# Lending query slots, input tiles and accumulators to a heap of exponential blocks

## The chip, the core and the metric

The kernel runs on one core of one Trainium2 chip. A core has five engines that run side by side and wait for each other by semaphores: TensorE (PE, matrix products, with its weight loads shown as PEld), ScalarE (ACT, functions of single elements), VectorE (DVE), GpSimd (POOL) and SyncE (SP, which here issues DMAs). Compute engines work on SBUF, 128 partitions; matmuls write PSUM, eight banks of 128x512 fp32. The metric is the time of one execution on the device, in microseconds.

## What is computed

Four layers with a residual each: `x = x + A(LN(x)); x = x + B(LN(x)); x = x + A(LN(x)); x = x + B(LN(x))`, for 2048 rows of 512 elements, with the same weights in both A layers and in both B layers.

```python
def A(x, wq, wk, wv, wo):          # 32 query heads of 16, ONE key and value head
    q = heads(x @ wq); k = x @ wk; v = x @ wv
    p = softmax(q @ k.T * 16 ** -0.5)          # 32 x 2048 x 2048
    return merge(p @ v) @ wo
def B(x, wqkv, wo):                # linear attention, 32 heads of 16
    q, k, v = split(x @ wqkv)
    phi = lambda t: where(t > 0, t + 1, exp(t)) + 1e-6
    kv = phi(k).T @ v; z = phi(k).sum(rows)
    return merge(phi(q) @ kv / (phi(q) @ z + 1e-6)) @ wo
```

Layers 0 and 2 are of kind A, layers 1 and 3 of kind B. Nearly all of the work is the softmax of the A layers.

## The kernel before

**A planner writes the order.** The program isn't a loop over tiles but a small event simulation (`Planner`) that runs while the program is built. Every piece of a layer is a Python generator that waits for flags, takes a PSUM bank or a buffer from a pool, and then calls `op` with an engine, an assumed duration, a priority and the keys it reads and writes. The planner gives each engine the ready operation of least priority number and so fixes each engine's order; at the end it emits these orders with semaphore waits that follow from the keys. The assumed durations only shape the order. On the chip each engine works through its list in that order.

**Layers of kind A.** The 2048 rows are 16 tiles of 128. `ln_tile` normalizes a tile and transposes it into `xnT` (features on partitions), by DMA for tiles 4 to 15 and by TensorE for the first. `a_k`, `a_v` and `a_q` project keys, values and queries (`mm4` at line 966 issues 16 matmuls for a tile's queries, `copy_flex` at line 780 copies the bank to `QT`, one slot of 128x512 for each tile). The keys lie in `KM` twice, each copy masked to half of the rows, so that a matmul over 32 rows gives the scores of one head: "par" is the half, j the group of 32 rows.

A segment (`Seg`) is a query tile and a half: 16 key tiles times four groups j, 64 blocks of 128 keys by 512 columns (four heads' worth of 128 queries). A layer has 32 segments' worth of blocks, 2048; the first tiles of a layer are cut into shorter pieces (`E0`, `E2`), so that work can begin before all keys are there, and their sums are kept in `sacc`, one fp32 accumulator for each tile and half. `act_stream` walks the segments in rounds. A round takes a set of three PSUM banks; up to three score matmuls (line 1051) fill them, and ScalarE makes one exponential of two or three banks (line 1240). Where two are enough for ScalarE, the third bank goes to VectorE (`dve_split`), and where a bank is spare VectorE gets one more (`dve_open`). VectorE does the exponential as integer arithmetic on the bits of a bf16 (line 1344). Four such blocks are a chunk; GpSimd adds a constant to a chunk three times (`int64_add`, line 1386), which shifts the approximation's phase, and the four versions are weighted and summed by four value matmuls (`VW`) in place of one (`V`, both line 1105). VectorE blocks are allowed from the eighth key tile on (`KGATE`), are picked from the back of a segment, and only if enough blocks lie ahead.

**The heap.** All exponentials, VectorE blocks and shifted copies live in `W`, a tile of 72 blocks of 128x512 bf16 handed out by `Heap_`, lowest number first. A block is held until its value matmul. Four rules look at how many are free: ScalarE's `take` needs its blocks and four more (`RES`), a new VectorE chunk more than 8 (`FBO`), a shift that isn't urgent more than 16 (`FBS`), and a value matmul with fewer than four column groups is held back while 14 or more are free (`LOW`).

**Value matmuls and the end of a segment.** Value matmuls go segment by segment into bank 6, four column groups at a time. Then VectorE copies the bank to `sacc` (lines 1407 and 1409), TensorE transposes it (1429), VectorE divides (1436, 1440), and `epilogue` transposes, multiplies by `wo` and adds to `x_sb`. Fillers (line 1150) are matmuls with zeros that TensorE runs when it has nothing else to do.

**Layers of kind B** run tile by tile under the attention of their neighbours: `tile_` normalizes into `xnT` and projects keys and values, `q_` projects queries into `QT` and applies phi (line 1516 on ScalarE, 1517 and 1519 on VectorE), `kv_`/`kvt` build the products, `main`/`main3` finish a tile. phi(k) lies in `pk`, which is a view of `sacc` 2 to 5.

**When queries are projected.** In layer 0 all tiles are projected as soon as their input is there. In layer 2 tiles 5 to 15 wait for a segment's end (`QHOLD`, `QHC`). In layer 1 tiles 4 to 13 wait until layer 0's exponentials are all planned (`QLATE`, flag `exps`).

## Time and profile before

| what | value |
|---|---|
| time, median of 3 runs | 1393.46 us (1390.98 to 1452.55) |
| the profiled execution | 1391.23 us, of which the span is 1389.3 us |
| busy: TensorE / ScalarE / VectorE / GpSimd | 1344.2 / 1347.3 / 1216.5 / 1033.0 us |
| granted TensorE clock, mean | 0.999 |
| DMA | 20.58 MB, mean 15 GB/s |

The span runs from the first to the last instruction of the profiled execution. A row of a group gives the line, the engine and operation, the tile written and read, the number of instructions, then their busy time together, the mean time of one in ns, and the idle time of the engine just before them with what ended most of it. Instructions overlap in their engine's pipeline, so the busy time of a group is less than the count times the mean. A row of waits gives the total in us, the number of waits and the longest. A row of windows gives the stretch, its length and the busy time with the number of instructions for each engine, then the granted clock, the DMA share and GB/s.

### The profile page before, as it was taken

The page shows a single profiled execution, that of the slowest core. Times are in us where ns is not written, and L with a number is a line of the kernel's source. Part 1 is how long each engine was busy: PE and PEld are TensorE (multiplying, and loading weights), DVE is VectorE, ACT ScalarE, POOL GpSimd, SP SyncE. Part 2 cuts the span into 40 slices and gives each one's busy share as a digit, 9 for nine tenths or more (in the row PEclk, how much of TensorE's full clock was granted, in tenths as well). Part 3 has the DMA queues.
Part 4 walks back from the last instruction along what each step waited for, and adds up shares of the span by engine and source line. Part 5 has one row for each costly group of instructions (what it writes and reads, how often), then busy time and mean ns, then how long its engine had stood idle before and what let it go on. Part 6 is the DMA issues. An engine that isn't in the chain of part 4 may idle for free.

```text
span 1389.3 us, 38426 instructions
## 1 busy us (share of the span) xinstructions
PE 1344.2 (97%) x15092; PEld 465.4 (33%) x15092; DVE 1216.5 (88%) x2184; ACT 1347.3 (97%) x1543; POOL 1033.0 (74%) x1031
## 2 busy tenths in 40 slices
PE   8999999999999999999999999999999999999998
PEld 5422222232222222233632333333333322223335
DVE  8889888898889988897889988988898899888977
ACT  8999999999999999999799999999999999999996
POOL 1489998778979998776005878867888799977770
PEclk9999999999999999999999999999999999999999
DMA  4300000000000000000021000000000000000001
GB/s 108 93 6 5 6 6 20 6 13 2 10 9 6 5 6 13 2 1 3 5 51 36 5 5 9 21 6 6 13 6 9 5 6 5 6 13 2 2 2 62
DMA packets 52465, 20.58 MB, mean 15 GB/s; under 512 B 46144, under 2 KB 51776, under 8 KB 52288
## 3 DMA queue, kind: packets, MB, share of 16 engines
q1 hardware_dynamic: 51232, 18.10, 5.7%
q8 instruction: 122, 2.00, 0.6%
q14 instruction: 55, 0.45, 0.1%
q10 hardware_dynamic: 1056, 0.03, 0.0%
HBM read 5.28 MB, written 2.10 MB: 5 GB/s over the span
## 4 chain that ended last, share of the span: by engine, by line
PE 52%; ACT 29%; DVE 9%; issue 7%; POOL 1%; DMA 1%; SPq 0%; ACTq 0%; DVEq 0%; POOLq 0%
ACT W L1240 28%; PE ps L1105 20%; PE ps L1051 17%; PE ps L786 6%; DVE W L1344 5%; PE ps L966 3%; PE ps L1429 2%; PE ps L1150 2%; POOL W L1386 1%; ACT phE L1516 1%; DVE phE L1517 1%; DVE sacc L1407 1%; DVE xn L884 1%; DMA x_sb<-in_A_x_dram 1%; DVE st L871 0%
## 5 line engine op out<-in xcount | busy, mean ns | idle before, releaser
L1240 ACT ACTIVATE W<-ps 128x1024 bf16<-128x1024 f32 (+1 forms) x1332 | 1287.5, 1157 | 11.5 <-PE ps L1051 8.4
L1386 POOL INT64_ADD W<-W x999 | 1027.4, 1041 | 314.7 <-DVE W L1344 156.8
L1344 DVE TENSOR_SCALAR W<-ps 128x512 int16<-128x512 f32 x1332 | 868.8, 683 | 121.8 <-PE ps L1051 106.5
L1105 PE MATMUL ps<-W,VW 128*32 128x512 bf16 x5328 | 562.4, 384 | 7.5 <-DVE sacc L1407 7.1
L1051 PE MATMUL ps<-QT,KM 32*128 32x512 bf16 x4096 | 520.7, 385 | 23.9 <-ACT W L1240 12.9
L1105 PE MATMUL ps<-W,V 128*32 128x512 bf16 x2764 | 447.7, 384 | 0.0
L1051 PEld LDWEIGHTS ps<-QT,KM 32*128 32x128 bf16 x4096 | 130.5, 91 | 508.0 <-ACT W L1240 444.6
L1105 PEld LDWEIGHTS ps<-W,VW 128*32 128x32 bf16 x5328 | 133.7, 94 | 177.6 <-issue 115.8
L1105 PEld LDWEIGHTS ps<-W,V 128*32 128x32 bf16 x2764 | 108.0, 94 | 71.2 <-issue 46.7
L786 PE MATMUL ps<-wqkv,xnT 128*128 128x512 bf16 (+1 forms) x272 | 76.1, 371 | 1.7 <-DVE sacc L1519 1.5
L1150 PE MATMUL ps<-QT,V 128*32 128x512 bf16 (+4 forms) x278 | 74.1, 333 | 0.9 <-DVE QT L780 0.8
L1516 ACT ACTIVATE phE<-ps 128x512 bf16<-128x512 f32 (+1 forms) x66 | 43.5, 663 | 6.8 <-PE ps L966 6.7
L1407 DVE COPY sacc<-ps 128x512 f32<-128x512 f32 x64 | 43.6, 681 | 6.0 <-PE ps L1105 5.9
L1429 PE MATMUL ps<-identF,sacc 128*128 128x128 f32 x256 | 46.0, 292 | 1.6 <-DVE sacc L1519 0.8
L871 DVE BATCH_NORM_STATS2 st<-x_sb 128x6 f32<-128x512 bf16 x60 | 40.5, 680 | 0.6 <-DMA x_sb<-in_A_x_dram 0.3
L884 DVE TENSOR_SCALAR xn<-x_sb,mv,rs 128x512 bf16<-128x512 bf16 x64 | 35.6, 571 | 2.2 <-ACT rs L862 2.0
L966 PE MATMUL ps<-xnT,wqkv 128*128 128x128 bf16 x512 | 37.4, 220 | 0.0
L1517 DVE TENSOR_SCALAR phE<-phE 128x512 bf16<-128x512 bf16 (+1 forms) x66 | 33.2, 506 | 4.5 <-ACT phE L1516 4.1
L786 PE MATMUL ps<-wo,OT 128*128 128x512 bf16 x120 | 36.0, 384 | 0.9 <-DVE QT L1519 0.5
L966 PE MATMUL ps<-xnT,wq 128*128 128x128 bf16 x464 | 35.2, 220 | 0.0
L1429 PEld LDWEIGHTS ps<-identF,sacc 128*128 128x128 f32 x256 | 27.6, 142 | 19.9 <-issue 14.3
L1150 PEld LDWEIGHTS ps<-QT,V 128*32 128x32 bf16 x278 | 22.7, 95 | 29.7 <-issue 15.6
(140 smaller groups left out, 599.0 us busy)
## 6 DMA issues: line engine op xcount, KB each, us to landing
out_dram<-x_sb SPq DMA_DIRECT2D x16, 128.0 KB, 1.7
x_sb<-in_A_x_dram SPq DMA_DIRECT2D x6, 256.0 KB, 5.4
wqkv<-in_B_wqkv_dram SPq DMA_DIRECT2D x1, 1536.0 KB, 7.9
xnT<-xn SPq DMA_TRANSPOSE x46, 2.5
x_sb<-in_A_x_dram SPq DMA_DIRECT2D x4, 128.0 KB, 2.2
wq<-in_A_wq_dram SPq DMA_DIRECT2D x1, 512.0 KB, 4.2
wo<-in_A_wo_dram SPq DMA_DIRECT2D x1, 512.0 KB, 4.1
wo<-in_B_wo_dram SPq DMA_DIRECT2D x1, 512.0 KB, 8.8
```

Source lines behind the costliest of these rows:

```text
L786: return e.matmul(dst, lhsT=l, rhs=r, start=(k == 0), stop=(k == len(pairs) - 1))
L884: op({DV: (0.325, lambda e: e.tensor_scalar(out=xn[:, i, :], in0=x_sb[:, t, :], scalar1=mv[:, t, 0:1], scalar2=rs[:, t:t + 1], op0=ALU.sub ...
L966: ins = e.matmul(dst[:, g * P:(g + 1) * P], lhsT=lhs(g, k), rhs=rhs(k), start=(k == 0), stop=(k == FT - 1))
L1051: return e.matmul(bank(b), lhsT=KM[r, sg.par, kt * P:(kt + 1) * P], rhs=QT[r, sg.t, :], start=True, stop=True)
L1105: ins = e.matmul(ps[32 * j:32 * j + 32, ACC * 512:(ACC + 1) * 512], lhsT=V[:, kt, :] if w is None else VW[:, kt, w, :], rhs=ap, start=(k = ...
L1150: o = op({PE: (n / 2400.0, lambda e: e.matmul(ps[32 * j:32 * j + 32, b * 512:b * 512 + n], lhsT=V0[:], rhs=QT[:, sg.t, 0:n], start=st, sto ...
L1240: ex = op({AC: (EXO + 0.4267 * n, lambda e, n=n, s_=s_, p_=p_: e.activation(ws_(p_), ps[:, s_ * 512:(s_ + n) * 512], ACTF.Exp, scale=EXPSC ...
L1344: o = op({DV: (0.602, lambda e: e.tensor_scalar(out=dst.bitcast(I16), in0=bank(b), scalar1=VB, scalar2=VLO, op0=ALU.add, op1=ALU.max))}, w ...
L1386: o = op({PO: (512 * m * PSR + PSO, lambda e, g_=g_, f_=f_: e.int64_add(ws_(g_).bitcast(I64), ws_(f_).bitcast(I64), step))}, reads=wk_(f_) ...
L1407: o = op({DV: (0.6, lambda e, src=src: e.tensor_copy(src, bank(ACC)))}, writes=[B_(ACC), key], prio=0.0, lat=0.15)
L1429: o = op({PE: (0.12, lambda e, c=c: e.transpose(ps[:, b * 512 + c * P:b * 512 + (c + 1) * P], src[:, c * P:(c + 1) * P], identF[:]))}, rea ...
L1516: op({AC: (0.07 + n / 1200.0, lambda e: e.activation(phE[:, i, 0:n], bank(b, n), ACTF.Exp))}, reads=[B_(b)], writes=[("phE", i)], prio=pr ...
```

## The change

All of the lendable memory is put into one tile with the heap. `W` grows from 72 blocks to 108: 16 are the query slots (`QT` becomes a view of them), 16 the normalized inputs (`XT`, which replaces `xnT` and has one block of four 128x128 pieces for each tile, so that a tile's inputs lie together), and four are two of the eight fp32 accumulators (units 6 and 7; `sacc` shrinks to six). The memory in total is the same.

A lendable block is at home, in use by its owner, or lent. `lend` hands it to the heap, `lend_after` does so when a flag is there and its last readers are done, and `recall` takes it back: if it is free at once, else when the heap releases it, asked every 0.2 us of the planner's time.

- Layer 0: query slots 4 to 15 and the four accumulator blocks are lent from the start. A tile's queries are now projected only when the value matmuls of segment 2t+2 are all issued, six segments ahead of its first own segment. Slots 4 to 13 are lent again after the tile's last segment. The accumulator blocks are recalled when the layer's exponentials are planned.
- Layer 1's queries recall their slots. When a tile of layer 1 is finished, slots 5 to 15 are lent until layer 2's queries.
- Layer 2: the accumulators 6 and 7 are lent once they are transposed for the last time. Inputs of layer 3's tiles 0 to 13 are lent after their last projection.

The constants of the heap's rules stay as they are.

```diff
     def free(self, heap, blocks):
-        heap.free.update(blocks)
+        heap.home.update(heap.back.intersection(blocks))
+        heap.free.update(set(blocks) - heap.back)
...
 class Heap_:
     def __init__(self, n):
-        self.n = n
+        self.n = n + 2 * T + 4
         self.free = set(range(n))
+        self.home = set(range(n, self.n))
+        self.back = set(self.home)
...
+LEND0 = range(4, 16)
+QLEAD = 6
+XLEND = 14
...
-    xnT = sb("xnT", [P, FT, S], BF16)
-    QT = sb("QT", [P, T, D], BF16)
...
-    W = sb("W", [P, NW, 512], BF16)
+    W = sb("W", [P, NW + 2 * T + 4, 512], BF16)
+    QT = W[:, NW:NW + T, :]
+
+    XT = W[:, NW + T:NW + 2 * T, :].rearrange("p t (f s) -> p t f s", f=FT)
+    SB0 = NW + 2 * T
...
-    sacc = sb("sacc", [P, 8, 512], FP32)
+    sacc = sb("sacc", [P, 6, 512], FP32)
+
+    def acc_(u):
+        if u < 6:
+            return sacc[:, u, :], [("sacc", u)]
+        b = SB0 + 2 * (u - 6)
+        return W[:, b:b + 2, :].rearrange("p a b -> p (a b)").bitcast(FP32), [("W", b), ("W", b + 1)]
...
             yield ("flag", ("K", L, T - 1))
             if QHC is not None:
                 yield ("flag", ("pv", L, QHC + 2 * (t - QHOLD[L][0])))
-        yield from until(("xnT", t))
+        if L == 0 and t in LEND0:
+            i = 2 * len(E0) + 2 * (t - 2) - QLEAD
+            if i >= 0:
+                yield ("flag", ("pv", L, i))
+        yield from recall(NW + t)
+        yield from until(XK_(t))
...
+    def lend(b):
+        heap.back.discard(b)
+        heap.home.discard(b)
+        pl.free(heap, [b])
+
+    def lend_after(key, b):
+        def g():
+            yield ("flag", key)
+            yield ("ops", list(pl.readers.get(("W", b), ())) + pl.ws(("W", b)))
+            lend(b)
+        pl.process(g())
+
+    def recall(b):
+        heap.back.add(b)
+        if b in heap.free:
+            heap.free.discard(b)
+            heap.home.add(b)
+        while b not in heap.home:
+            yield ("sleep", 0.2)
+
+    def shares():
+        for t in LEND0:
+            lend(NW + t)
+        for i in range(4):
+            lend(SB0 + i)
+        yield ("flag", ("exps", 0))
+        for i in range(4):
+            yield from recall(SB0 + i)
...
             if sg.submitted == sg.total:
                 pl.flag(("pv", L, sg.i))
+                if sg.last and sg.par and L == 0 and sg.t in QLATE[1]:
+                    lend_after(("pv", L, sg.i), NW + sg.t)
...
             if a_ is not None:
                 pl.give_after(as_pool, a_, [o])
+            elif L == 2 and sg.unit >= 6:
+                for i in range(2):
+                    lend_after(("pv", L, sg.i), SB0 + 2 * (sg.unit - 6) + i)
...
             if t in QLATE[L]:
                 yield ("flag", ("exps", L - 1))
-            yield from until(("xnT", t))
+            yield from recall(NW + t)
+            yield from until(XK_(t))
...
             pl.give_after(bq_pool, s_, [o])
+            if L == 3 and t < XLEND:
+                yield ("flag", ("kvin", L, t))
+                lend_after(("pkin", L, t), NW + T + t)
             pl.flag(("bq", L, t))
...
             pl.flag(("x", L, t))
+            if t in QHOLD[2]:
+                lend_after(("x", L, t), NW + t)
```

Everywhere else, `xnT[:, k, t * P:(t + 1) * P]` becomes `XT[:, t, k, :]` and the keys `("xnT", t)` and `("QT", t)` become the heap's `("W", b)`. A key matmul over several tiles reads `XT[:, t0:t0+n, ft, :]`, n pieces of 128 columns.

More of the change, by code (lines that the diff above doesn't have):

```diff
@@ L752, in setup @@
         yield ("flag", ("Q", 0, 1))
-        yield from until(("QT", 0))
+        yield from until(QK_(0))
         pool_op(lambda e: e.memset(identF[:], 0.0), ["identF"], prio=1.0)
@@ L926, in a_v @@
             yield ("flag", ("xnT", L, t))
-        yield from until(*[("xnT", t) for t in ts])
+        yield from until(*[XK_(t) for t in ts])
         b = yield ("acq", banks, prio)
@@ L945, in a_k @@
             yield ("flag", ("xnT", L, t))
-        yield from until(*[("xnT", t) for t in ts])
+        yield from until(*[XK_(t) for t in ts])
         n = P * len(ts)
@@ L949, in a_k @@
         b = yield ("acq", banks, prio)
-        mm(bank(b, n), [(wkr[:, ft, :], xnT[:, ft, cs]) for ft in range(FT)], [("xnT", t) for t in ts] + ["wkr"], b, prio, 4 * (0.02 + n / 2500.0))
+        mm(bank(b, n), [(wkr[:, ft, :], XT[:, ts[0]:ts[0] + len(ts), ft, :]) for ft in range(FT)], [XK_(t) for t in ts] + ["wkr"], b, prio, 4 * (0.02 + n / 2500.0))
         last = None
@@ L1424, in norm @@
             yield ("flag", ("oslot", L, sg.t))
-            yield from until(key)
+            yield from until(*key)
             b = yield ("acq", banks, pr)
@@ L1561, in tile_ @@
                 yield ("flag", ("kv", L, t // 4 - 2))
-            yield from until((EB if t in ECRIT else "xnT", t))
+            yield from until((EB, t) if t in ECRIT else XK_(t))
             if t in ECRIT:
@@ L1570, in tile_ @@
             b = yield ("acq", banks, pr)
-            mm(bank(b), [(xnT[:, ft, t * P:(t + 1) * P], wqkv[:, ft, D:2 * D]) for ft in range(FT)], [("xnT", t), "wqkv"], b, pr, 0.9)
+            mm(bank(b), [(XT[:, t, ft, :], wqkv[:, ft, D:2 * D]) for ft in range(FT)], [XK_(t), "wqkv"], b, pr, 0.9)
             pl.process(phi_k(t, b, sl, pr))
@@ L1574, in tile_ @@
             b = yield ("acq", banks, pr)
-            mm(bank(b), [(xnT[:, ft, t * P:(t + 1) * P], wqkv[:, ft, 2 * D:3 * D]) for ft in range(FT)], [("xnT", t), "wqkv"], b, pr, 0.9)
+            mm(bank(b), [(XT[:, t, ft, :], wqkv[:, ft, 2 * D:3 * D]) for ft in range(FT)], [XK_(t), "wqkv"], b, pr, 0.9)
             src, dst = bank(b).rearrange("p (h d) -> p h d", d=DH), va_v[:, sl, :, 0:DH]
@@ L1693, in den3 @@
                 yield ("flag", ("bq", L, t))
-            yield from until(*[("QT", t) for t in ts], *ZK)
+            yield from until(*[QK_(t) for t in ts], *ZK)
             i = yield ("acq", rd_pool, pr)
@@ L1837, in main @@
                 yield ("flag", ("xnT", 2, MW[t]))
-                yield from until(("xnT", MW[t]))
+                yield from until(XK_(MW[t]))
             i = yield ("acq", ob_pool, pr)
```

64 lines of the change are left out of this document (35 added, 29 removed).

## The prediction

> **What bounds the kernel now.** I first read the page's busy times, its chain and its costliest groups, to see which engine paces the attention layers.
>
> ```profile
> PE 1344.2 (97%) x15092; PEld 465.4 (33%) x15092; DVE 1216.5 (88%) x2184; ACT 1347.3 (97%) x1543; POOL 1033.0 (74%) x1031
> ...
> PE 52%; ACT 29%; DVE 9%; issue 7%; POOL 1%; DMA 1%; SPq 0%; ACTq 0%; DVEq 0%; POOLq 0%
> ACT W L1240 28%; PE ps L1105 20%; PE ps L1051 17%; PE ps L786 6%; DVE W L1344 5%; PE ps L966 3%; PE ps L1429 2%; PE ps L1150 2%; POOL W L1386 1%; ACT phE L1516 1%; DVE phE L1517 1%; DVE sacc L1407 1%; DVE xn L884 1%; DMA x_sb<-in_A_x_dram 1%; DVE st L871 0%
> ...
> L1240 ACT ACTIVATE W<-ps 128x1024 bf16<-128x1024 f32 (+1 forms) x1332 | 1287.5, 1157 | 11.5 <-PE ps L1051 8.4
> L1386 POOL INT64_ADD W<-W x999 | 1027.4, 1041 | 314.7 <-DVE W L1344 156.8
> L1344 DVE TENSOR_SCALAR W<-ps 128x512 int16<-128x512 f32 x1332 | 868.8, 683 | 121.8 <-PE ps L1051 106.5
> L1105 PE MATMUL ps<-W,VW 128*32 128x512 bf16 x5328 | 562.4, 384 | 7.5 <-DVE sacc L1407 7.1
> ```
>
> The softmax exponentials are shared out in blocks of 128x512, 4096 in all. ScalarE (L1240) takes two or three blocks in one instruction. VectorE (L1344) takes single blocks, 1332 of them, and GpSimd (L1386) makes three shifted copies of every four. A VectorE block therefore needs 5328/1332 = 4 value matmuls where a ScalarE block needs one. TensorE and ScalarE are both 97% busy, so the share must be read by stage. The next answer gives the busy time of every engine over stretches of the two attention layers (seven columns: PE, weight loads, DVE, ACT, POOL, clock, DMA).
>
> ```profile
> 50.00:100.00 50.00, 49.05 (x590) 17.53 (x587) 43.69 (x74) 50.00 (x54) 41.72 (x41) 1.00 0.02 4
> 100.00:250.00 150.00, 145.60 (x1663) 42.38 (x1660) 134.86 (x228) 148.80 (x165) 142.03 (x140) 1.00 0.05 9
> 250.00:410.00 160.00, 156.08 (x1716) 48.66 (x1714) 138.77 (x238) 158.71 (x178) 128.39 (x126) 1.00 0.04 8
> 410.00:540.00 130.00, 126.06 (x1483) 36.96 (x1483) 114.52 (x193) 130.00 (x143) 123.96 (x122) 1.00 0.03 6
> 540.00:650.00 110.00, 107.94 (x1154) 33.27 (x1154) 97.78 (x172) 109.63 (x125) 84.53 (x83) 1.00 0.02 4
> 720.00:1120.00 400.00, 386.95 (x4338) 128.58 (x4337) 356.28 (x614) 394.11 (x442) 305.99 (x297) 1.00 0.06 12
> 1120.00:1220.00 100.00, 96.79 (x1154) 28.08 (x1150) 90.87 (x155) 100.00 (x112) 97.16 (x97) 1.00 0.03 7
> 1220.00:1350.00 130.00, 125.08 (x1356) 40.18 (x1355) 113.93 (x191) 126.68 (x145) 100.76 (x97) 0.99 0.02 4
> sum 1230.00, PE 1193.54 PEld 375.64 DVE 1090.68 ACT 1217.92 POOL 1024.53; mean PE 149.19 PEld 46.95 DVE 136.34 ACT 152.24 POOL 128.07
> ```
>
> ScalarE is busy for 1217.92 of 1230 us, in every stretch. Two kinds of stretch differ in what else is full. From 100 to 250, 410 to 540 and 1120 to 1220 GpSimd is full as well (142.03 of 150, 123.96 of 130, 97.16 of 100): this is attention alone. In the others linear-layer work is mixed in, and GpSimd idles for about a fifth of the time. Some of TensorE's time is filler (L1150, matmuls of zeros issued when it has nothing else):
>
> ```profile
> 100.00:250.00 150.00, 14.31 (x54) 4.37 (x54) 1.00 0.05 9
> 250.00:410.00 160.00, 8.08 (x31) 2.56 (x31) 1.00 0.04 8
> 540.00:650.00 110.00, 1.29 (x4) 0.29 (x4) 1.00 0.02 4
> ...
> sum 1230.00, PE 66.18 PEld 20.39; mean PE 8.27 PEld 2.55
> ```
>
> So TensorE has room in the first kind of stretch (14.31 us in 150) and almost none from 540 to 650. The pace is ScalarE's, with TensorE close behind. The time can then fall in one way mainly: blocks must go from ScalarE to VectorE. How many could? The exponentials by shape, first over the span, then from 10 to 50, 680 to 720 and 1120 to 1170 us:
>
> ```profile
> L1240 ACT ACTIVATE W<-ps 128x1024 bf16<-128x1024 f32 x1228 | 1157.8, 1126 | 9.8 <-PE ps L1051 8.4
> L1240 ACT ACTIVATE W<-ps 128x1536 bf16<-128x1536 f32 x102 | 151.0, 1534 | 1.8 <-PE ps L1105 1.8
> ...
> L1240 ACT ACTIVATE W<-ps 128x1536 bf16<-128x1536 f32 x14 | 20.6, 1473 | 0.0
> ...
> L1240 ACT ACTIVATE W<-ps 128x1536 bf16<-128x1536 f32 x15 | 22.2, 1477 | 0.0
> ...
> L1240 ACT ACTIVATE W<-ps 128x1024 bf16<-128x1024 f32 x55 | 50.9, 1128 | 0.0
> ```
>
> A three-bank exponential (128x1536) is a round in which VectorE took no block of the set. There are 102; 14 and 15 of them lie at the starts of the two layers, where VectorE isn't let in yet (the key gate), which leaves 73. In the best stretch there is none: 55 two-bank rounds in 50 us.
>
> **What a block is worth.** A two-bank exponential takes 1157.8/1228 = 0.943 us of ScalarE, so a block moved off it saves 0.471 us. It costs VectorE 868.8/1332 = 0.652 us and GpSimd 1027.4/1332 = 0.771 us. For TensorE the value matmuls over the whole span are needed:
>
> ```profile
> 0.00:1390.00 1390.00, 617.41 (x8092) 149.60 (x8092) 1.00 0.06 15
> ```
>
> 617.41/8092 = 0.0763 us each; three more make 0.229 us. Over the 1230 us above, VectorE has 139 us idle, GpSimd 205 us, and TensorE 36 us idle and 66 us of filler. Twenty more blocks would take 13, 15 and 4.6 us of these, so on average there is cover, though not in every stretch.
>
> **The change, part by part.**
>
> *The heap.* It has 72 blocks. In layer 0 it gets 12 query slots and four half-accumulator blocks more, 88 at the start. By the code about four of the 12 slots are in use at a time, three tiles projected ahead and the one being consumed, which leaves some 84. In layer 2 it gets 11 slots, which go back as queries are projected, and later up to 14 input tiles and the four blocks. Is the heap what refuses blocks now? A full heap would show as exponentials or shifts that wait until value matmuls (L1105) release a block. First for the whole span, then for 720 to 1120:
>
> ```profile
> POOL W L1386 <- DVE W L1344: 156.8, 115, 43.4
> ...
> POOL W L1386 <- PE ps L1105: 31.7, 23, 5.1
> ...
> ACT W L1240 <- PE ps L1051: 8.4, 19, 1.8
> ...
> ACT W L1240 <- PE ps L1105: 1.8, 4, 0.6
> ...
> POOL W L1386 <- PE ps L1105: 24.0, 14, 5.1
> ```
>
> ScalarE almost never waits for a block: 1.8 us. GpSimd does: 31.7 us in 23 waits, 24.0 us of it in layer 2's long mixed stretch, where GpSimd is not the bound. That is the one place where scarcity shows by itself. The 31.7 us would be 31.7/0.771 = 41 blocks, worth 19.4 us, if VectorE filled them all. The bounds of the whole term: nothing, if what comes in their place is GpSimd's larger wait, the one for VectorE (156.8 us); and all 73 three-bank rounds turned, 73 x 0.471 = 34.4 us. I take half of the 41, 20 blocks: a shift that starts sooner sometimes only waits longer to be consumed, and where GpSimd is already full (142.03 of 150) a larger heap can only store chunks once, not add any per microsecond. That is 20 x 0.471 = 9.4 us.
>
> The Trainium skill (Perfetto Trace Analysis, section Optimization Strategy) says that one gap repeating on the engine that should be saturated can mean that there isn't space enough for the next tile. On ScalarE the trace shows no such gap (1.8 us in four waits), so by that rule space would not be what limits this kernel and the sum would be 0 instead of 9.4 us; the waits that speak for space are on GpSimd.
>
> *Queries of layer 0.* Tiles 4 to 15 are now projected one per two segments instead of all before 80 us. Before, the matmuls from 20 to 80 us, and the copies of the layer:
>
> ```profile
> L966 PE MATMUL ps<-xnT,wq 128*128 128x128 bf16 x192 | 14.7, 220 | 0.0
> ...
> L780 DVE CAST QT<-ps 128x512 bf16<-128x512 f32 x15 | 10.2, 678 | 1.0 <-PE ps L966 1.0
> ```
>
> These 192 matmuls are exactly 12 tiles: 14.7 us of TensorE, 12 x 0.678 = 8.1 us of VectorE. Nothing is added or removed; no DMA moves with them. VectorE's first block starts here:
>
> ```profile
> L1344 DVE TENSOR_SCALAR W<-ps x1332: 625/681/694, 47.5 to 1345.8; 128x512 int16<-128x512 f32 x191
> ```
>
> From 47.5 to 80 us the freed 8.1 us could hold 12 more blocks (8.1/0.652), 5.7 us; the same 8.1 us is missing later. Where GpSimd is the limit (100 to 250, 410 to 540) it costs nothing; in the mixed stretch it may cost those 12 blocks again. I take 0 and keep 5.7 us on both sides. A query too late would stall the whole stream, but its flag is six segments ahead: a layer's 32 segments take about 640 us, 20 us each, so 120 us. A lent slot comes home when its block is consumed; in 50 us there pass through the heap some 54 exponentials (x54 from 50 to 100), 108 blocks, and 1332 x 50/1230 = 54 VectorE blocks with their copies, 216, together 6.5 per us, so one of 88 blocks is held for about 13.5 us. Some 100 us are left; I cost it at 0.
>
> *Between layers 0 and 1.* Slots 4 to 13 are lent again when their segments end, and layer 1's queries wait for their return. Before, from 640 to 660 us:
>
> ```profile
> 640.00:660.00 20.00, 3.81 (x56) 3.22 (x56) 1.00 0.01 3
> ```
>
> The matmuls that now would have to wait for the last value matmuls are at most these 3.81 us. What comes after is full, so they'd be late by that much: 0 to 4 us; I take 0, since low blocks are given out first and the lent ones return first when the heap drains.
>
> *The rest.* The tile-major layout of the inputs, the strided key matmuls and the accumulators in the heap's tile keep every instruction's elements. Nothing in the trace prices the other stride; all of this work lies beside ScalarE's exponentials. 0, within 2 us either way.
>
> The sum: 1391.2 (the profiled execution, 1389.3 of span and 1.9 around it) - 9.4 = 1382 us. That execution is 2.2 us under the median of the runs shown.
>
> **The rivals.**
>
> *Nothing moves:* the extra blocks stay empty or hold blocks longer. For it: ScalarE's 1.8 us, and GpSimd's main wait being for VectorE. Against it: the 31.7 us. Time 1391, give or take 3. This also covers a change that lends but doesn't use.
>
> *The heap is the limit throughout:* the 73 rounds turn. They need 47.6 us of VectorE and 56.3 of GpSimd, both there on average. Against it: no wait on ScalarE shows it, and where linear work takes VectorE's time a round is refused for VectorE's own queue. 1391.2 - 34.4 = 1357.
>
> *TensorE becomes the bound (slower):* four of the moved queries (one per 40 us) fall from 250 to 410, 4 x 14.7/12 = 4.9 us, and 20 blocks bring 4.6 us of value matmuls. Where filler is gone (1.29 us in 110) neither has cover; from there on ScalarE waits for scores, and what it saves is lost. 1391.2 + 9.5 = 1401. Against it: 8.08 us of filler in just that stretch.
>
> **How the numbers follow.** Forecast 0.50, nothing moves 0.22, the heap throughout 0.10, TensorE the bound 0.15; 0.03 for a stall of the stream that none of these has, over 28 us. The range is 1366 to 1397. Its low end is 1382 less half of the 25 us to the heap rival (12.5) and about half of what the queries may give (3); its high end is nothing gained and the queries' 5.7 us lost (1391.2 + 5.7). Most of the heap rival, half of TensorE's case and the stall lie outside, about 2 in 10. A measurement of this kernel can tell some 2%, 28 us, from no change. Faster by that needs 59 blocks: most of the heap rival, 0.10. Slower by that: the stall and the far end of TensorE's case, 0.05. Within: 0.85.
>
> **What would show it.** Right: more VectorE instructions at L1344's line than 1332, about 1350, with three more GpSimd adds for every four; fewer three-bank exponentials between 50 and 650 and 720 and 1350; GpSimd's wait for value matmuls well under 31.7 us; query matmuls spread from 80 to 520 us. Wrong: 1332 blocks as before (nothing moves); more than about 1390 (the heap throughout); ScalarE's wait for scores well over 8.4 us with no filler left (TensorE); a wait of exponentials for query copies (the stall).

## The result: 0.3% slower

| | before | after |
|---|---|---|
| median of 7 runs each, same chip | 1392.17 us | 1396.20 us |
| span of the profiled execution | 1389.3 us | 1394.5 us |
| ratio of after to before, 95% interval | | 1.0033 [1.0022, 1.0044] |

The forecast was 1382 us, 0.7% faster. The measured time lies in its range, on the other side of before. Lines move: 1240 becomes 1299, 1344 becomes 1403, 1386 becomes 1445, 1105 becomes 1162, 1051 becomes 1108, 884 becomes 905, 786 becomes 807, 966 becomes 987.

The page of after, its busy times, chain and costliest groups:

```profile
PE 1334.8 (96%) x15056; PEld 468.6 (34%) x15134; DVE 1225.5 (88%) x2192; ACT 1344.3 (96%) x1544; POOL 1042.6 (75%) x1043
...
PE 53%; ACT 25%; DVE 11%; issue 7%; POOL 3%; ACTq 0%; POOLq 0%; DVEq 0%
...
L1299 ACT ACTIVATE W<-ps 128x1024 bf16<-128x1024 f32 (+1 forms) x1329 | 1280.8, 1154 | 9.3 <-PE ps L1108 7.9
L1445 POOL INT64_ADD W<-W x1011 | 1037.0, 1037 | 302.7 <-DVE W L1403 117.6
L1403 DVE TENSOR_SCALAR W<-ps 128x512 int16<-128x512 f32 x1344 | 878.3, 685 | 105.5 <-PE ps L1108 90.7
```

VectorE took 12 blocks more (1344 for 1332), GpSimd 12 adds more, and ScalarE's exponentials fell from 1287.5 to 1280.8 us. Six of the 12 blocks lie in the first 50 us, where VectorE has fewer queries to copy (its blocks there, first before, then after):

```profile
0.00:50.00 50.00, 1.98 (x3) 1.00 0.53 139
0.00:50.00 50.00, 5.50 (x9) 0.97 0.51 138
```

The waits and the exponentials by shape, of after:

```profile
POOL W L1445 <- DVE W L1403: 117.6, 116, 8.0
...
POOL W L1445 <- PE ps L1162: 19.0, 16, 3.3
ACT W L1299 <- PE ps L1108: 7.9, 24, 0.6
```
```profile
L1299 ACT ACTIVATE W<-ps 128x1024 bf16<-128x1024 f32 x1235 | 1164.1, 1125 | 7.8 <-PE ps L1108 6.9
L1299 ACT ACTIVATE W<-ps 128x1536 bf16<-128x1536 f32 x94 | 140.0, 1536 | 1.4 <-PE ps L1108 0.9 <-PE ps L1162 0.4
```

GpSimd's wait for a block to come free fell from 31.7 to 19.0 us, and the three-bank rounds from 102 to 94. So more blocks, a shorter wait and the later queries are there as forecast. One sign is not: the three-bank rounds were to fall from 50 to 650 us and from 720 to 1350. In the first stretch there are 32 in before and 33 in after, in the second 38 and 36:

```profile
L1240 ACT ACTIVATE W<-ps 128x1536 bf16<-128x1536 f32 x32 | 47.5, 1544 | 1.2 <-PE ps L1105 1.2
L1299 ACT ACTIVATE W<-ps 128x1536 bf16<-128x1536 f32 x33 | 49.3, 1555 | 0.0
```

And the time rose. Where did it go? The exponentials' own rows around the change of layers (start, length, count; VectorE's blocks end with them), first before, then after:

```profile
649.56 5.72 ACT L1240 ACTIVATE W<-ps 128x1024 bf16<-128x1024 f32 x5
679.93 1.02 ACT L1240 ACTIVATE W<-ps 128x1024 bf16<-128x1024 f32 x1
```
```profile
645.99 4.16 ACT L1299 ACTIVATE W<-ps 128x1536 bf16<-128x1536 f32 x3
683.32 1.02 ACT L1299 ACTIVATE W<-ps 128x1024 bf16<-128x1024 f32 x1 [0.48 <-PE ps L1108]
```

Layer 0's exponentials end 5.1 us earlier (650.15 for 655.28), and layer 2's begin 3.4 us later: the gap in which there is only linear work grew from 24.65 to 33.17 us. Layer 2's stretch takes 668.25 us for 672.19, and the tail behind the last exponential 42.93 for 37.18. The sum: -5.1 + 8.5 - 3.9 + 5.7 = +5.2 us, which is the difference of the spans. **The attention got shorter by 9 us, close to the 9.4 forecast, and the linear work left over behind it grew by 14 us.** That 9 comes so near 9.4 is in part luck: the exponentials themselves lost 6.7 us (1287.5 to 1280.8), about what 12 blocks are worth at the prediction's 0.471 us each, and not what 20 are.

What was left over? The normalisations of layer 1's tiles on VectorE from 520 to 610 us, first before, then after, where the statistics of the next two tiles were both ready at 516.15:

```profile
525.96 0.86 DVE L884 TENSOR_SCALAR xn<-x_sb,mv,rs 128x512 bf16<-128x512 bf16 x1
539.17 1.13 DVE L884 TENSOR_SCALAR xn<-x_sb,mv,rs 128x512 bf16<-128x512 bf16 x1
542.18 0.31 DVE L884 TENSOR_SCALAR xn<-x_sb,mv,rs 128x512 bf16<-128x512 bf16 x1
546.40 0.40 DVE L884 TENSOR_SCALAR xn<-x_sb,mv,rs 128x512 bf16<-128x512 bf16 x1
599.25 0.40 DVE L884 TENSOR_SCALAR xn<-x_sb,mv,rs 128x512 bf16<-128x512 bf16 x1
604.12 0.99 DVE L884 TENSOR_SCALAR xn<-x_sb,mv,rs 128x512 bf16<-128x512 bf16 x1
```
```profile
446.21 2.16 DVE L905 TENSOR_SCALAR xn<-x_sb,mv,rs 128x512 bf16<-128x512 bf16 x2
606.55 0.41 DVE L905 TENSOR_SCALAR xn<-x_sb,mv,rs 128x512 bf16<-128x512 bf16 x1
```
```profile
515.98 0.17 DVE L893 BATCH_NORM_AGGREGATE mv<-st 128x2 f32<-128x6 f32 x1
```

For 158 us after places none. Before has such a pause too, of 138 us, but it ends at 526 us. After's ends at 607, and so three of layer 1's normalisations start in the last 15 us of layer 0's exponentials, where before starts none; the last ones, first before, then after:

```profile
632.05 1.26 DVE L884 TENSOR_SCALAR xn<-x_sb,mv,rs 128x512 bf16<-128x512 bf16 x1
635.93 1.51 DVE L905 TENSOR_SCALAR xn<-x_sb,mv,rs 128x512 bf16<-128x512 bf16 x2
639.59 0.44 DVE L905 TENSOR_SCALAR xn<-x_sb,mv,rs 128x512 bf16<-128x512 bf16 x1
```

What runs instead is seen on GpSimd (busy time in stretches of 20 us), first before, then after:

```profile
540.00:560.00 20.00, 14.84 (x16) 1.00 0.07 15
560.00:580.00 20.00, 16.30 (x16) 1.00 0.01 2
```
```profile
540.00:560.00 20.00, 19.55 (x21) 1.00 0.01 2
560.00:580.00 20.00, 19.25 (x20) 1.00 0.01 2
```

In the code the normalisation and the adds both carry `port=True`, and the planner holds a normalisation back while its book has an add running. With adds back to back there is hardly a moment when it isn't so. Layer 1's key and value matmuls wait for their tiles: their weight loads, first before, then after:

```profile
560.00:610.00 50.00, 1.90 (x32) 1.00 0.01 2
...
650.00:660.00 10.00, 0.00 (x0) 1.00 0.01 2
```
```profile
560.00:610.00 50.00, 0.31 (x4) 1.00 0.02 4
...
650.00:660.00 10.00, 2.23 (x24) 1.00 0.01 2
```

They run in the gap (52 weight loads in all of it, for 32 in before's). TensorE was not short of time meanwhile: filler from 540 to 650 rose from 1.29 us to

```profile
540.00:650.00 110.00, 7.67 (x29) 2.53 (x29) 1.00 0.01 3
```

The tail has more of layer 3's query projections in it, by their weight loads after the last exponential, first before, then after:

```profile
L966 PEld LDWEIGHTS ps<-xnT,wqkv 128*128 128x128 bf16 x80 | 4.9, 99 | 0.3 <-DVE sacc L1519 0.2
```
```profile
L987 PEld LDWEIGHTS ps<-W,wqkv 128*128 128x128 bf16 x106 | 6.6, 99 | 1.1 <-DVE sacc L1581 0.3
```

The cause isn't the gap's: layer 3's normalisations lie much as in before (the last two start at 1332 and 1358 us, for 1336 and 1358). Why its queries came later isn't known.

### The profile page after: what moved, and what is told of

It reads as the page before. It is cut to its first block, busy times and chain, and to the rows that moved or that the text cites. A ratio compares the mean times of both kernels' runs of the same rounds, so it can differ in the third digit from the quotient of the medians.

```text
span 1394.5 us, 38437 instructions
## 1 busy us (share of the span) xinstructions
PE 1334.8 (96%) x15056; PEld 468.6 (34%) x15134; DVE 1225.5 (88%) x2192; ACT 1344.3 (96%) x1544; POOL 1042.6 (75%) x1043
## 4 chain that ended last, share of the span: by engine, by line
PE 53%; ACT 25%; DVE 11%; issue 7%; POOL 3%; ACTq 0%; POOLq 0%; DVEq 0%
ACT W L1299 24%; PE ps L1162 21%; PE ps L1108 17%; PE ps L807 5%; DVE W L1403 4%; PE ps L987 3%; POOL W L1445 3%; PE ps L1488 2%; PE ps L1209 2%; DVE xn L905 1%; DVE phE L1579 1%; DVE sacc L1466 1%; DVE sacc L1581 1%; ACT phE L1578 0%; DVE st L892 0%
## 5 line engine op out<-in xcount | busy, mean ns | idle before, releaser
L1299 ACT ACTIVATE W<-ps 128x1024 bf16<-128x1024 f32 (+1 forms) x1329 | 1280.8, 1154 | 9.3 <-PE ps L1108 7.9
L1403 DVE TENSOR_SCALAR W<-ps 128x512 int16<-128x512 f32 x1344 | 878.3, 685 | 105.5 <-PE ps L1108 90.7
L1108 PE MATMUL ps<-W,KM 32*128 32x512 bf16 x4096 | 519.3, 384 | 25.3 <-ACT W L1299 14.9
L1108 PEld LDWEIGHTS ps<-W,KM 32*128 32x128 bf16 x4096 | 130.3, 91 | 504.7 <-ACT W L1299 437.2
L1162 PEld LDWEIGHTS ps<-W,V 128*32 128x32 bf16 x2752 | 105.3, 94 | 81.3 <-issue 56.1
L1209 PE MATMUL ps<-W,V 128*32 128x512 bf16 (+4 forms) x298 | 77.4, 336 | 1.4 <-DVE x_sb L1976 0.6
L807 PE MATMUL ps<-wqkv,W 128*128 128x512 bf16 (+1 forms) x233 | 64.9, 367 | 7.3 <-issue 3.7
L1488 PE MATMUL ps<-identF,sacc 128*128 128x128 f32 x248 | 43.8, 290 | 0.9 <-DVE sacc L1581 0.8
L987 PE MATMUL ps<-W,wqkv 128*128 128x128 bf16 x512 | 36.9, 220 | 0.1
L987 PE MATMUL ps<-W,wq 128*128 128x128 bf16 x464 | 35.4, 220 | 0.5 <-DVE W L1581 0.5
L807 PE MATMUL ps<-wo,OT 128*128 128x512 bf16 x90 | 29.2, 382 | 5.9 <-issue 3.3
L1209 PEld LDWEIGHTS ps<-W,V 128*32 128x32 bf16 x298 | 23.8, 95 | 30.4 <-issue 14.3
```

Of the source, the lines that this page charges most:

```text
L807: return e.matmul(dst, lhsT=l, rhs=r, start=(k == 0), stop=(k == len(pairs) - 1))
L987: ins = e.matmul(dst[:, g * P:(g + 1) * P], lhsT=lhs(g, k), rhs=rhs(k), start=(k == 0), stop=(k == FT - 1))
L1108: return e.matmul(bank(b), lhsT=KM[r, sg.par, kt * P:(kt + 1) * P], rhs=QT[r, sg.t, :], start=True, stop=True)
L1162: ins = e.matmul(ps[32 * j:32 * j + 32, ACC * 512:(ACC + 1) * 512], lhsT=V[:, kt, :] if w is None else VW[:, kt, w, :], rhs=ap, start=(k = ...
L1209: o = op({PE: (n / 2400.0, lambda e: e.matmul(ps[32 * j:32 * j + 32, b * 512:b * 512 + n], lhsT=V0[:], rhs=QT[:, sg.t, 0:n], start=st, sto ...
L1299: ex = op({AC: (EXO + 0.4267 * n, lambda e, n=n, s_=s_, p_=p_: e.activation(ws_(p_), ps[:, s_ * 512:(s_ + n) * 512], ACTF.Exp, scale=EXPSC ...
```

## The experiments

The expectations name theories by letters. **A**: linear work is displaced, because the larger heap keeps GpSimd's adds unbroken and the planner then never places a normalisation. **B**: the new layout costs. **Late slots**: the gap grows because the query slots lent to the end of layer 0 come home late. **C**: the heap's size isn't the limit, 72 blocks are enough. **D** and **E** came later: before is one lucky order among many, or orders are alike.

All results in one table, from the profiled execution of each: VectorE's blocks, three-bank rounds, then in us the two stretches of exponentials together (up to layer 0's last, and layer 2's), the gap and the tail together, and their sum, the span. The ratio is to before, measured on the same chip, from several executions; a span is of one execution, up to 3 us from the median of its run.

| run | blocks | 3-bank | exponentials | gap + tail | span | ratio [95%] |
|---|---|---|---|---|---|---|
| before | 1332 | 102 | 1327.5 | 61.8 | 1389.3 | 1 |
| after | 1344 | 94 | 1318.4 | 76.1 | 1394.5 | 1.0033 [1.0022, 1.0044] |
| e1 layout | 1332 | 102 | 1327.5 | 61.8 | 1389.3 | 0.9998 [0.9987, 1.0009] |
| e2 layer 0 | 1332 | 103 | 1327.3 | 68.0 | 1395.3 | 1.0048 [1.0033, 1.0063] |
| e3 layer 2 | 1340 | 95 | 1317.9 | 73.1 | 1391.0 | 1.0023 [1.0013, 1.0032] |
| e4 no re-lending | 1339 | 93 | 1321.5 | 73.0 | 1394.5 | 1.0035 [1.0022, 1.0048] |
| e5 after, turns 2 | 1335 | 96 | 1331.0 | 61.2 | 1392.2 | 1.0009 [0.9998, 1.002] |
| e6 before, turns 2 | 1324 | 108 | 1345.6 | 59.5 | 1405.1 | 1.0104 [1.009, 1.0119] |
| e7 after, adds free | 1347 | 100 | 1342.7 | 60.2 | 1402.9 | 1.0091 [1.0078, 1.0105] |
| e8 before, adds free | 1319 | 136 | 1338.8 | 62.3 | 1401.1 | 1.0093 [1.008, 1.0107] |
| e9 before, 66 blocks | 1283 | 151 | 1347.4 | 61.0 | 1408.4 | 1.0138 [1.0116, 1.0159] |
| e10 queries just in time | 1315 | 119 | 1334.9 | 69.2 | 1404.1 | 1.0109 [1.0085, 1.0133] |
| e11 after, turns 3 | 1345 | 81 | 1323.3 | 62.4 | 1385.7 | 0.9962 [0.9947, 0.9977] |
| e12 e4, turns 3 | 1343 | 83 | 1324.6 | 60.9 | 1385.5 | 0.999 [0.9979, 1.0002] |
| e13 before, 0.61 | 1299 | 135 | 1341.5 | 60.8 | 1402.3 | 1.0088 [1.007, 1.0106] |
| e14 before, 0.59 | 1320 | 119 | 1326.1 | 72.0 | 1398.1 | 1.0058 [1.0038, 1.0077] |
| e15 after, 0.61 | 1341 | 91 | 1322.9 | 71.5 | 1394.4 | 1.0038 [1.0027, 1.005] |
| e16 lent, early queries | 1330 | 96 | 1332.4 | 62.8 | 1395.2 | 1.0043 [1.0031, 1.0055] |
| e17 before, turns 3 | 1314 | 117 | 1348.1 | 61.8 | 1409.9 | 1.0142 [1.0125, 1.0159] |
| e18 e16, turns 3 | 1344 | 79 | 1324.2 | 62.4 | 1386.6 | 0.9993 [0.9984, 1.0002] |

### Parts alone (e1 to e4)

e1, the layout without any loan and without the just-in-time queries:

```diff
-LEND0 = range(4, 16)
+LEND0 = ()
...
-            lend(SB0 + i)
...
-                if sg.last and sg.par and L == 0 and sg.t in QLATE[1]:
+                if False:
...
-            elif L == 2 and sg.unit >= 6:
+            elif False:
...
-            if L == 3 and t < XLEND:
+            if False:
...
-            if t in QHOLD[2]:
+            if False:
```

> Everything of the change is in but the lending and the just-in-time queries: one tile for heap, queries, inputs and two accumulators, tile-major inputs, strided key matmuls, and no block is ever lent, so that every engine's order should be that of the kernel before. Theory A (displaced work: the larger heap lets the exponentials push linear-layer work out of the attention stretch into the gap behind it) expects the time of before within 0.2%, with 655 us to the end of layer 0's last exponential and 25 us from there to layer 2's first. Theory B (the new layout costs by itself, in strides or in the DMA transposes) expects some 4 us more than before.

e2 keeps layer 0's part alone (the last three `False`); e3 layer 2's alone (the other edits).

> Only layer 0 lends (query slots 4 to 15 with their just-in-time projection, and the four accumulator blocks); nothing is lent in layer 2. Theory A expects layer 0 as in the changed kernel: last exponential at about 650 us, gap of about 33 us, layer 2 starting 3 to 4 us later than before; then layer 2 and the end near those of before (672 and 37 us), so about 1392 to 1395 us. A theory by which layer 0's lending gains and layer 2's loses expects less than before.

> Only layer 2 lends (slots 5 to 15 after layer 1, inputs of layer 3, two accumulators); layer 0 is as before, queries early. Theory A expects layer 0 as before (655 us, gap 25 us) and the pattern of the changed kernel in layer 2: exponentials 4 us shorter or more (672 to 668 us), the stretch after the last one 6 us longer or more (37 to 43 us). A theory by which only layer 0's end is hurt expects a time below before by those 4 us.

e4 is after with only the re-lending of slots 4 to 13 gone:

```diff
-                if sg.last and sg.par and L == 0 and sg.t in QLATE[1]:
+                if False:
```

> The changed kernel, but slots 4 to 13 of layer 0 are not lent again when their segments end, so layer 1's queries never wait for a slot to come home. The rival that the prediction priced at 0 to 4 us (late slots lengthen the gap) expects the gap of 33 us back at 25 us with layer 0's exponentials still ending near 650 us. Theory A expects the gap to follow the key and value projections instead: it shrinks only if more of the normalisations (line 905) get in before 600 us; with these still absent from 450 to 600 us the gap stays above 30 us.

B falls: e1 has before's counts and time. Layer 0's part alone has after's gap of 33.17 us; layer 2's alone has a longer tail (48.5 us). Without the re-lending the gap is back (25.28 us), but so are the normalisations (four from 500 to 600 us, none in after), and the tail grew to 47.7: that run alone can't tell late slots from A.

### Turns for the normalisation (e5 to e8, e11, e12)

A normalisation that has been ready for `PWAIT` us makes GpSimd's next add wait, and goes first. e5 is this on after and e6 on before, with 2 us:

```diff
+PWAIT = 2.0
...
+            if e == DV and self.port <= self.now:
+                old = [y for y in h if y[2].port and y[2].eng is None and self.now - y[2].since > PWAIT]
...
+            if e == PO and o.port and any(y[2].port and y[2].eng is None and self.now - y[2].since > PWAIT for y in self.ready[DV]):
+                held.append(x)
```

> The changed kernel with all its lending and re-lending, and one rule more in the planner: once a VectorE operation that the planner keeps apart from GpSimd's adds (the flag port) has been ready for 2 us, GpSimd's next add is held until it has been placed, and VectorE takes it first. Theory A, now with its mechanism (the larger heap keeps GpSimd's row of adds unbroken, so that the normalisations of line 905 never find a place in the order) expects normalisations between 500 and 600 us again, the gap after layer 0 back near 25 us with re-lending kept, the end after layer 2 back near 37 us, most of the shorter exponential stretches kept, and so 4 to 10 us less than the kernel before: 1381 to 1387 us. The rival of the late slots expects the gap to stay at 33 us, and about 1396 us.

> The same rule of turns in the kernel before, with its heap of 72 blocks. Theory A expects little: its normalisations found places already (four from 500 to 550 us), so within 4 us of the kernel before. If the rule of turns is worth as much here as in the changed kernel, then the larger heap gives nothing and the gain belongs to the rule alone.

e7 (after) and e8 (before) let adds and normalisations overlap freely:

```diff
-                       reads=wk_(f_), writes=wk_(g_), prio=pr, lat=0.15, port=True)
+                       reads=wk_(f_), writes=wk_(g_), prio=pr, lat=0.15)
```

> The changed kernel with the flag port taken off GpSimd's adds, so that the planner places the VectorE operations of lines 905 and 1579 beside adds as if nothing were shared. Theory A expects the gap and the end to be short as with turns. What the chip then does is open: a normalisation beside an add took 1 us and more where one without took 0.4 us, 64 of them and 66 of line 1579, so up to some 80 us more of VectorE, spread over the attention; if that counts, the time is above that of the run with turns, else below.

> The flag taken off the adds in the kernel before. Theory A expects no gain of the size that the changed kernel has from it, since nothing was starved here: within 5 us of the kernel before. It serves as the pair to the same edit in the changed kernel.

e11 is after with `PWAIT = 3.0`, e12 the same without re-lending.

> The changed kernel with the rule of turns, but after 3 us of waiting instead of 2: a second sample of the same idea, since every edit reshuffles the whole order. Theory C expects the time of the kernel before within 0.4%, with gap and end near 25 and 36 us. Theory A in its first form (the shorter stretches of exponentials are kept) expects 1381 to 1387 us. If a VectorE normalisation falls into a row of adds and is held for over 2 us, TensorE's clock drops and the time is longer by some 4 us for each such place.

> As the run before it, and in addition slots 4 to 13 aren't lent again at the end of layer 0. A third sample. The rival of the late slots expects this to be faster than the run with re-lending by a shorter gap; theories A and C expect the gaps of the two to agree within 2 us.

Late slots fall: e5 and e11 re-lend as after does, and the gap is 26.0 us in both (and 25.3 in e15 below, without turns). A is half right. With the normalisations placed, the gap and tail are back at 61.2, but in e5 the exponentials took 1331.0 us, more than before's (e5's executions spread from 1388.3 to 1394.1 us, and the profiled one took 1394.0). So part of after's 1318.4 may have been short only because linear work had left the stretch; e5 also has nine blocks fewer than after, so this isn't shown. With 3 us the exponentials kept 4.2 us of the gain (1323.3), and e11 is faster than both kernels, at 1386.41 us. But the same rule made before 1% slower (e6), where A forecast a change within 4 us, and e5 lies 5 us above the 1381 to 1387 that A forecast for it; A doesn't explain either.

### Size of the heap and queries (e9, e10)

```diff
-    NW = 72
+    NW = 66
```

> The kernel before with a heap of 66 blocks instead of 72, nothing else. Theory C (72 blocks are about enough: the heap's size isn't what limits the number of VectorE blocks, so more of it gives nothing once the displaced work is back under the attention, as the run with turns showed) expects a small loss here, some 0.3%, or 4 us. The rival that the prediction took (VectorE blocks are refused for want of heap) expects six blocks fewer to cost what twelve or more gain, half of 9 us or more, with clearly fewer than 1332 VectorE blocks and more than 73 three-bank exponentials outside the starts of the layers; a loss of 1% or more here, beside no gain above 72, would mean a knee near 72.

e10 has the layout and the just-in-time queries (`LEND0` kept for them), and lends nothing.

> The changed kernel without any lending: layer 0's queries of tiles 4 to 15 are projected just in time, and that is all. The prediction priced this at 0, within 5.7 us. If the just-in-time part were what displaces the linear work of layer 1, the gap after layer 0 would be near 33 us here too and no normalisation would lie between 500 and 600 us; theory A (the unbroken row of adds that the larger heap allows) expects normalisations there and a gap near 25 us. Time within 6 us of the kernel before.

C falls if e9 is read at face value: six blocks fewer cost 1.4%, and GpSimd's wait for blocks rose to

```profile
POOL W L1386 <- PE ps L1105: 49.3, 31, 5.3
```

so it reads 49.3, 31.7 and 19.0 us for 66, 72 and up to 88 blocks. But e10, which was expected within 6 us of before, costs 1.1% with the same 72 blocks, and 9.4 us of the 14.8 that its span is longer lie behind layer 2's first exponential (718.7 us to the end, for before's 709.4), where its code differs from before's only by the layout, which e1 had shown to cost nothing. Something that belongs to neither edit was at work.

### The order itself (e13 to e18)

e13, e14 and e15 change nothing but a duration that the planner assumes for VectorE's copy to the accumulators and its add to them, by 10 ns (the copy is shown). No operation is edited; the order, and with it the split of blocks, changes.

```diff
-                    o = op({DV: (0.6, lambda e, src=src: e.tensor_copy(src, bank(ACC)))}, writes=[B_(ACC), key], prio=0.0, lat=0.15)
+                    o = op({DV: (0.61, lambda e, src=src: e.tensor_copy(src, bank(ACC)))}, writes=[B_(ACC), key], prio=0.0, lat=0.15)
```

> Before, with the planner's assumed duration of the accumulator copies 0.61 us in place of 0.60 (no instruction changes, only the order that the planner writes). Theory D (before is a lucky order among many that 72 blocks allow): slower than before by 6 to 15 us (1398 to 1407), with other counts of VectorE blocks and 3-bank exponentials. Theory E (orders are alike, the change itself costs): within 3 us of before (1389 to 1395).

> Before, with that duration 0.59 us. Theory D: again 6 to 15 us slower than before, by another split between the stages than in the run with 0.61. Theory E: within 3 us of before.

> After, with that duration 0.61 us. Theory D: anywhere from 1386 to 1402, and below the two nudged kernels of before by 5 us or more, since the lent heap still takes more blocks (1340 or more VectorE blocks). Theory E: within 3 us of after (1393 to 1399).

Before became 0.88% slower by the one and 0.58% by the other; after stayed at 1396.7, which taken alone fits E and is only 3 us under e14, where D asked for 5. VectorE's blocks in e13:

```profile
L1344 DVE TENSOR_SCALAR W<-ps 128x512 int16<-128x512 f32 x1299 | 850.5, 685 | 122.6 <-PE ps L1051 107.7 <-POOL W L1386 1.6 <-ACT phE L1516 0.4
```

And e14, which lends nothing, has after's gap, and three normalisations in the last 15 us of layer 0's exponentials, behind some 80 us without one. Its exponentials, and GpSimd just before they end:

```profile
641.68 9.17 ACT L1240 ACTIVATE W<-ps 128x1024 bf16<-128x1024 f32 x8
684.77 1.45 ACT L1240 ACTIVATE W<-ps 128x1536 bf16<-128x1536 f32 x1 [0.82 <-PE ps L1051]
```
```profile
600.00:620.00 20.00, 19.41 (x20) 1.00 0.01 2
620.00:640.00 20.00, 20.00 (x20) 1.00 0.01 2
```

E falls by e13 and e14, and D holds so far: the gap of 33.9 us is something that an order can have with 72 blocks too. e16 is after with early queries (`LEND0 = ()`, the accumulators and later loans kept), e18 the same with turns of 3 us, e17 before with those turns.

> After without the just-in-time queries: the query slots of tiles 4 to 15 are not lent at the start and their queries are projected as early as before; the accumulators, the slots that come free when their tile is done, and all of layer 2's loans stay. If just-in-time projection is a cost of its own (10 us or more): 1380 to 1387, and layer 0's exponentials end before 650 us. If it costs nothing (Theory D): 1388 to 1402, with layer 0 no shorter than in after (650 us).

> Before (72 blocks) with the turns that wait 3 us. If the lent blocks carry the gain of the kernel with turns on after (1386): here 1395 to 1405, as the nudged kernels of before, with 1335 VectorE blocks or fewer. If the turns carry it: 1383 to 1390.

> After without the just-in-time queries and with the turns that wait 3 us. If the lent blocks carry the gain: 1383 to 1392, and 1340 VectorE blocks or more. If the kernel with turns on after was only a lucky order: anywhere up to 1402. If the just-in-time queries had given the blocks that count: 1392 to 1400.

e17 is the slowest of all 72-block orders; e18 comes within 0.07% of before. So it isn't the turns alone that made e11 fast; e18 fits both the lent blocks and a lucky order. And just-in-time queries have no price that shows beside loans: 1396.2 with them and 1396.8 without (after, e16), 1386.4 and 1389.7 with turns (e11, e18).

**Reading all orders together.** Seven orders use 72 blocks with nothing lent (before, e6, e8, e10, e13, e14, e17; e1 has before's order), eleven lend something (after, e2 to e5, e7, e11, e12, e15, e16, e18). Their means: 1318 and 1340 blocks, 119 and 92 three-bank rounds, spans of 1401.4 and 1392.5 us, ratios of 1.0085 and 1.0024. The difference of the ratios is 0.61%, with a 95% interval of 0.2 to 1.0% if the orders are taken as drawn at random, which they weren't. Before is the fastest of its seven, and the next is 0.58% behind. In pairs with the same planner, lent minus not: +0.33% (as given), -0.50% (0.61), -0.95% (turns 2), -1.80% (turns 3), -0.02% (adds free); mean -0.59%, with a 95% interval from -1.6 to +0.4%, so that the pairs alone don't settle the sign.

The difference lies where the heap should act: the exponentials take 1337.5 us on the mean of the seven and 1326.0 on that of the eleven, gap and tail 63.9 and 66.5. GpSimd's wait for blocks is 27.0 to 43.8 us in the seven, and 9.9 to 26.0 in ten of the eleven (52.9 in e5). But the orders are few and not alike: e13 and e14 differ from before, and e15 from after, by the nudge alone; most others change a rule of the planner, the loans or the time of the queries. With only before, after and the nudged orders the difference is small: ratios of 1, 1.0088 and 1.0058 without loans, 1.0033 and 1.0038 with.

## Why the prediction was wrong

*The heap: the direction holds on the mean of the orders, the size in this pair doesn't.* 20 blocks were forecast, worth 9.4 us. The means of the orders differ by 22 blocks and 8.9 us of span, with the wide intervals above; after itself has 12 more than before. Six of these lie before 50 us and need no loan: the nine orders with the later queries have 6 to 12 blocks there (e10, which lends nothing, has 10), the other eleven 2 to 4. GpSimd's wait for blocks fell to 60%, where half was assumed.

*The step that failed is to take all of before's order over and subtract the heap's gain from it.* In the measured pair it shows as two terms. "Between layers 0 and 1", taken as 0 within 0 to 4, measured +8.5 us, and the tail, which had no term at all, +5.7; together they outweigh the 9.1 us by which the attention got shorter. Behind them lies the base of the sum, "1391.2 (the profiled execution ...) - 9.4". It takes before's time as what 72 blocks give, so that a better heap must come out below it. The runs show that before is the best of seven orders, 12 us of span under their mean (1389.3 for 1401.4), while after lies 2 us above the mean of the eleven (1394.5 for 1392.5). Nothing in the one trace of before could show that; only a second order of the same kernel does. Whether before is a lucky draw or the planner's constants had been fitted to just this order, no run tells.

*The two terms.* For the gap the forecast looked for slots that come home late; what came late was layer 1's key and value work, behind normalisations that the planner had held back. In all twenty orders the gap follows these: it is 33.2 to 33.9 us in the three orders with three normalisations in the last 15 us of layer 0's exponentials (after, e2, e14), and 24.3 to 26.8 in the seventeen with one or none (the 15 us were picked on seeing the traces). That GpSimd's row of adds holds them back is read from the planner's rule and borne out by the turns, which bring gap and normalisations back to before's, and by e14, whose GpSimd was full from 600 to 640 us without loans. In e3 and e4, whose tails are the longest, four and five of layer 3's normalisations start in the last 15 us of exponentials; in after none does, and for its tail no cause was shown.

*Queries, 0 within 5.7:* not contradicted in after; e10, the only run with them and no loans, is 1.1% slower, which is no more than an order can differ by (e17 1.4%). The later queries did free VectorE before 50 us, for six blocks in after where the prediction allowed 12 up to 80 us. Their matmuls after the change, in layer 0, lie as forecast between 80 and 520 us:

```profile
20.00:80.00 60.00, 0.00 (x0) 0.00 (x0) 1.00 0.28 72
80.00:150.00 70.00, 2.48 (x32) 1.80 (x32) 1.00 0.08 9
...
250.00:400.00 150.00, 6.20 (x80) 4.49 (x80) 1.00 0.04 9
400.00:520.00 120.00, 4.79 (x64) 3.59 (x64) 1.00 0.03 7
```

*Layout, 0 within 2:* e1, 0.9998 [0.9987, 1.0009].

*The rivals.* "Nothing moves" gave 1391 and lies nearer than the forecast, but for a wrong reason: blocks moved and the rounds fell from 102 to 94. "The heap throughout" falls: 94 three-bank rounds remain. "TensorE becomes the bound" gave 1401, nearest of all, and the right sign, by luck: its marks are absent, ScalarE's wait for scores went from 8.4 to 7.9 us and filler grew where it should have gone.

What stays open: the tail, why one order gets 1345 blocks and another 1335 from the same loans (e11, e5), and why before's order is so good.

## What to carry to other kernels

Where a planner writes the order, one order is one draw: move an assumed duration by a per cent or two and measure a few draws of the old kernel before a difference under 1% is put down to an edit, and forecast against their mean. Read a gain in the bounding stretch together with the gap and the tail behind it, since a stretch may also get shorter because other work was pushed out of it. Where an operation may run only when another engine is idle, look for what happens when that engine never is.

## What was not expected of the hardware

Where the planner let a normalisation start beside a running row of adds (e7), the row of two normalisations and the row of adds around it, from VectorE's and GpSimd's timelines, and 5 us stretches (PE, weight loads, DVE, ACT, POOL, clock):

```profile
438.92 4.82 DVE L905 TENSOR_SCALAR xn<-x_sb,mv,rs 128x512 bf16<-128x512 bf16 x2
443.65 0.68 DVE L1403 TENSOR_SCALAR W<-ps 128x512 int16<-128x512 f32 x1
```
```profile
435.12 8.15 POOL L1445 INT64_ADD W<-W  x8
```
```profile
435.00:440.00 5.00, 5.00 (x69) 2.09 (x65) 4.86 (x9) 5.00 (x8) 5.00 (x6) 1.00 0.02 3
440.00:445.00 5.00, 0.86 (x10) 0.18 (x6) 5.00 (x5) 1.55 (x2) 3.27 (x4) 0.83 0.07 15
445.00:450.00 5.00, 5.00 (x36) 1.47 (x33) 3.37 (x6) 3.07 (x3) 2.12 (x3) 0.50 0.19 39
450.00:455.00 5.00, 5.00 (x39) 1.05 (x36) 2.89 (x5) 3.40 (x4) 1.50 (x2) 0.65 0.01 2
```

Alone a normalisation takes 0.40 us. Here VectorE was held until the whole row of adds was over (435.12 + 8.15 = 443.27), several adds of 1.04 us and not one; TensorE ran dry for some 4 us, and its granted clock then stood at half for about (0.85 + 2.5 + 1.75) / 0.5 = 10 us, from the shares missing in three stretches. The same is seen in all nine normalisations that took over 1.5 us (in e6, e7, e8, e14, e17 and e18): each ended 0.15 us behind the add at which GpSimd's row next broke off. Among these nine the clock fell only where TensorE ran dry: in e14 a normalisation was held for 4.32 us, TensorE stayed busy and its clock at 1.00. This is what the planner's rule avoids. In e7 it may be much of the loss (four normalisations held for 2.5 to 4.5 us, each with such a drop); e8 has only one, of 2.96 us, so most of its loss of 12 us has another cause. Neither was priced apart. The Trainium skill (SBUF — State Buffer, section Who interferes with whom) says, for VectorE instructions in a two-port mode, that whichever of the two engines issues first holds their shared port pair for its whole instruction while the other blocks fully. The trace agrees on the block, but not on its length: a row of back-to-back adds held it for all of the row. Which mode the normalisation ran in, no run here shows.
